# New step lists, thirteen copies on VectorE and an earlier start of the last weight combinations in a fused convolution and SiLU feed-forward kernel

## The chip, the cores and the metric

The kernel runs on one core of a Trainium2 chip. A core has TensorE (matmul), VectorE, ScalarE, GpSimd (here also called Pool) and a queue engine, SyncE (SP), that issues most DMA transfers. Each engine works through its own instructions in program order, and engines wait for one another by semaphores. On-chip memory is SBUF; matmul results land in PSUM, which has eight banks of 128 partitions by 512 fp32 values.

The metric is device time in microseconds (us). A profiled execution is taken by the hardware profiler; its times are those of one run.

## The reference, cut to what matters

```python
# x: (8, 4096, 192), weight: (8, 7), w_in: (192, 2048), w_out: (2048, 192), all fp32
w = softmax(weight, axis=-1)                    # 8 heads of 24 channels, 7 taps
x_pad = concat([zeros(B, 6, D), x], axis=1)
attn[b, s, h, c] = sum_k w[h, k] * x_pad[b, s + k, h*24 + c]
h = attn.reshape(32768, 192) @ w_in
out = (h * sigmoid(h)) @ w_out                  # fp32
```

A causal convolution with seven taps over the sequence, then an up product to 2048 features, SiLU, and a down product back to 192.

## The kernel before, in words

**Blocks.** The 32768 tokens are 32 blocks of 1024, two halves of 512 tokens each. For block b the kernel loads x (`load`, L270), transposes it on VectorE (`turn_in`, L533), gets the six tokens before it (`halo_in`, L548), convolves (`conv`, L561: the first tap on ScalarE, six on VectorE, for each of three groups of 64 channels), spreads the result by DMA into eleven slots of 64 rows on both partition halves (`spread`, L582), and forms sums and differences of slots (`win`, L596).

**Fast matrix products.** Block 0 uses plain matmuls (`up_plain`, `down_plain`). From block 1 on, both products are done with a scheme that needs fewer multiplications. The up product has 20 sub-products for each of four groups g of features (`product`, L644), each an fp32 matmul of 64 rows, 128 columns and 512 tokens; products on the upper and the lower 64 rows of the array (the first number in `PRODUCT`, 0 or 1) run side by side. They add into PSUM banks b0 to b6. Between them stand small steps (`micro`, L659): copies of a bank (kind "c": the u, k and h steps), additions and subtractions (kind "a": j and i steps, VectorE) and SiLU (kind "s": S steps, ScalarE). A copy of kind "c" goes to SBUF (u: a scratch tile; h: a hidden tile) or to another bank (k), and all 44 of a block (eleven kinds, four groups) are ScalarE's. The weights for this scheme are combined once at the start by Pool: `combine((0, 1), e)` and `combine((2, 3), e)` (L464), two groups of features at a time, 28 instructions for each pair of groups.

The down product has 48 slots a block (`out_slot`, L700), D*i*.*je*, each four matmuls on the four 32-column strips of the array, into banks acc0 to acc5. Eight of the 48 (D5) have 128 columns of tokens, the rest 512. Their inputs are hidden tiles and differences of them (`sum_g`, L683, the t steps, VectorE). The accumulators are then merged (`merge`, L769: z, y and x on ScalarE, M on VectorE), transposed (`turn_out`, o) and stored (`store_out`, st).

**The order of the work** is written out in two lists of tokens. `START` covers the first blocks, `PLAN` is one block of steady work and is run through once for each b from 3 to 33. A token names a step and its arguments: P8.2 is product 8 of group 2, D4.31 down slot 4 with j = 3, e = 1, v.26 convolution channel group 2, tap 6. A sign in front shifts the block: "+" is the next block, "-" the one before, "=" two before. `step` (L849) turns a token into its instructions. On each engine the instructions run in the order of the list; the order between engines comes from data alone. A token dp is one step of block 0's plain down product, cp copies its result, go starts the last combination of weights.

**Banks are handed round.** `at` (L257) gives an accumulator the next free bank, scratch tile or t tile when it is first touched, and takes it back after the number of touches in `TOUCHES`. A copy into a new bank can thus have to wait for the step that last read the bank's previous tenant, also where both are ScalarE's.

**The start.** After up_plain, Pool combines groups 0 and 1. The step go then issues a one-element copy out of the convolution tile of block 1 (L886) and, behind it on Pool's queue, the combination of groups 2 and 3. Last, `combine_out` (L476) prepares the down weights. The end (`finish`, L901) is not touched.

Of the kernel before, what the change touches and what calls it, by code (L numbers as in the profile page):

```python
# [17 lines left out]
def kernel(  # L18
# [47 lines left out]
        "ld.1 -st.3 i.1 j10.2 i18_10.2 ld.0 i17_f.2 ld.2 P14.2 t.03 P12.3 ze.0 j10.3 i18_10.3 "  # L66
        "S17.1 P14.3 D4.00 D4.01 D5.00 D1.31 i.0 S16.2 t.10 D5.01 i15_11.2 D3.00 D3.01 t.11 i.2 "
        "ha.0 t.13 i17_f.3 S15.2 t.12 D0.01 D0.21 v.00 t.20 D4.11 D4.10 D3.10 v.10 D2.10 v.20 "
        "v.01 v.11 v.21 S17.2 S18.2 D5.11 D2.11 v.02 t.21 v.22 t.23 v.23 v.03 D0.20 D1.10 D4.20 "
        "v.24 S13.3 i15_11.3 S17.3 D0.30 D4.21 v.04 D2.20 D3.11 D5.10 v.12 v.05 v.25 S15.3 D0.00 "  # L70
        "v.06 D2.21 D0.11 D0.10 t.22 D3.21 v.13 D5.21 D5.20 D0.31 D3.20 S18.3 D1.20 D1.30 D1.21 "
        "sp.0 D1.00 v.26 S16.3 v.14 v.15 z1.0 t.30 v.16 t.32 t.31 t.33 D2.30 D2.31 D5.30 D5.31 "
        "sp.2 y1.0 x2.1 D4.31 y0.0 sp.1 D3.30 D3.31 w.0 x2.2 w.1 w.2 w.3 w.4 x2.3 w.5 y2.0 x2.0 "
        "+P7.1 +P1.0 M1.0 +P7.0 +P1.1 x0.0 +h15.1 +k12.0 D4.30 +h15.0 M3.0 +k12.1 M2.0 x1.0 "
        "+h17.1 +P8.0 +u4.0 +P2.0 +P8.1 +P2.1 +P18.1 +P5.0 M4.0 +u4.1 +P17.1 +P5.1 +j4.0 +k5.0 "
        "+P16.0 +P3.0 +h17.0 M5.0 +k8.0 +P18.0 +P11.0 +P17.0 +S19.1 +k8.1 +P6.0 +u6.0 +h18.0 "
        "+P0.0 +P9.0 +u10.0 +j4.1 +S19.0 +P19.0 +k5.1 +P11.1 +P10.0 +P6.1 +P16.1 M6.0 M7.0 +P3.1 "
# [12 lines left out]
    START = (  # L90
        "-ld.0 =v.20 -ld.2 =v.00 =v.10 =v.01 =v.11 =v.12 =v.13 =dp.0 =dp.1 =dp.2 =dp.3 =dp.4 "
        "-ld.1 =dp.5 =dp.6 =dp.7 =dp.8 =dp.9 =dp.10 =dp.11 =dp.12 =dp.13 =dp.14 =dp.15 =dp.16 "
        "=dp.17 =dp.18 =dp.19 =dp.20 =dp.21 =v.02 =v.21 =dp.22 =v.22 =dp.23 =v.14 =dp.24 =v.23 "
        "=dp.25 =dp.26 =dp.27 =dp.28 =dp.29 =dp.30 =dp.31 =dp.32 =dp.33 =dp.34 =dp.35 =dp.36 "
        "=dp.37 =dp.38 =v.15 =v.03 =v.24 =v.25 =v.26 -i.2 =sp.2 =v.04 =v.05 =v.06 =sp.0 =dp.39 "
        "=dp.40 =dp.41 =dp.42 =dp.43 =dp.44 =dp.45 =dp.46 =v.16 -i.1 =sp.1 =w.1 =w.0 =cp.0 =go.2 "
        "-i.0 =w.2 -ha.0 =w.3 =w.4 =w.5 =dp.47 =cp.1 =o.1 -P1.1 =cp.2 =o.2 -k12.1 -P7.0 -P7.1 "
        "=st.2 -h15.0 -P2.1 -P7.3 -h17.1 -h15.1 -P1.0 -P8.0 -h15.3 -P8.1 -k12.0 -u4.0 -P2.0 "
        "-P17.1 -u4.1 -h17.0 -P5.0 -P18.1 -j4.0 =o.0 -P5.1 -P17.0 -k5.0 -S19.1 -P3.0 -j4.1 -P18.0 "
        "-k8.0 -P11.0 -P16.0 -u6.0 -S19.0 -j6.0 -P9.0 -P8.3 -h18.0 -k8.1 -P6.0 -P0.0 -S14.0 -P6.1 "  # L100
        "-k5.1 -P19.0 -u10.0 -P11.1 -P16.1 -S20.0 -k9.0 -P3.1 -P10.0 -u10.1 -P4.0 -h18.1 -P10.1 "
        "-i15_f.0 -u6.1 -P13.0 -u4.3 -P19.1 -j6.1 -S13.0 -i15_f.1 -P9.1 -P0.1 -k17.0 -k9.1 -j10.0 "
        "-P12.0 =st.1 =st.0 -P7.2 -S14.1 -S20.1 -P13.1 -P15.0 -i17_f.0 -h15.2 -P4.1 -S17.0 -P8.2 "
        "-i18_10.0 -k17.1 -P1.2 -S13.1 -P14.0 -j10.1 -u4.2 -P12.1 -P15.1 -k12.2 -i15_11.0 -S18.0 "
        "-P5.2 -j4.2 -h17.2 -i17_f.1 -P1.3 -S15.0 -P17.2 -i18_10.1 -S16.0 -P2.2 -k8.2 -P18.2 "
        "-t.00 -k12.3 -P6.2 -P14.1 -S17.1 -j4.3 -h17.3 -P11.2 -t.01 -S16.1 -P18.3 -P2.3 -S19.2 "
        "-u10.2 -P17.3 -i15_11.1 -P5.3 -k5.3 -t.03 -P10.2 -k5.2 -P3.3 -S19.3 -P16.3 -k8.3 "
        "-i15_f.2 -P3.2 -P16.2 -h18.3 -P11.3 -u6.2 -P0.3 -P6.3 -h18.2 -u6.3 -P0.2 -P9.2 -u10.3 "
        "-P19.2 -P9.3 -t.02 -j6.2 -j6.3 -k9.2 -S14.2 -P10.3 -k9.3 -P13.2 -S20.2 -P19.3 -S14.3 "
        "-P13.3 -i15_f.3 -k17.2 -P4.2 -S20.3 -P15.2 -k17.3 -P12.2 -v.00 -P15.3 -j10.2 -S13.2 "  # L110
        "-v.01 -S15.1 -D3.01 -i18_10.2 -v.10 -D4.01 -i17_f.2 -v.20 -v.11 -D1.01 -S18.2 -S17.2 "
        "-v.02 -D1.21 -j10.3 -D0.20 -v.03 -i18_10.3 -D0.10 -t.10 -S18.3 -D1.11 -v.12 -D0.00 -v.21 "
        "-D0.11 -v.13 -D1.31 -v.22 -v.14 -P14.2 -P4.3 -v.23 -P14.3 -P12.3 -S16.2 -v.15 -S13.3 "
        "-D1.20 -v.24 -S16.3 -S18.1 -i17_f.3 -D4.00 -v.16 -S17.3 -D3.00 -t.11 -sp.1 -D1.30 -ze.0 "
        "-i15_11.2 -D2.11 ld.1 -i15_11.3 -S15.2 -D2.01 -v.25 -S15.3 -D5.00 -v.04 -D5.01 -D0.21 "
        "-t.12 -D0.30 -D2.00 -t.13 -D2.10 -t.20 -D4.10 -v.05 -D3.10 -t.21 -D4.11 -v.06 -D5.11 "
        "-D5.10 -D2.20 -t.23 -sp.0 -D3.11 -v.26 -D4.20 -t.30 ld.0 -D5.21 -D5.20 -D4.21 -t.31 "
        "-D2.21 -t.22 -sp.2 -D2.31 -t.33 -D1.10 -D3.20 -t.32 ld.2 -D0.01 -D3.31 -w.0 -D5.30 "
        "-D3.30 -w.1 -D4.30 -w.2 -D0.31 i.2 -D3.21 -z1.0 -y0.0 -D5.31 -D1.00 -x0.0 -x2.3 -w.3 "
        "-w.4 -w.5 -D2.30 -y1.0 -x2.1 -D4.31 -x2.0 -M1.0 -x2.2 -M2.0 P7.1 P1.0 -x1.0 -M3.0 h15.1 "  # L120
        "-M4.0 k12.0 P1.1 P7.0 P8.1 -M5.0 h15.0 P2.0 -M7.0 k12.1 P8.0 -o.1 P2.1 h17.1 u4.0 -o.3 "
        "P18.1 u4.1 P5.0 j4.0 -st.3 P17.1 j4.1 h17.0 k5.0 P5.1 P17.0 S19.1 P3.0 -st.1 i.1 k8.0 "
        "P16.0 -y2.0 P11.0 k8.1 P18.0 -M6.0 h18.0 P11.1 u10.0 P19.0 u6.0 P6.0 u10.1 P10.0 P9.0 "
        "S19.0 j6.0 P10.1 k5.1 i15_f.0 P6.1 S14.0 P0.0 -o.0 k9.0 P3.1 i15_f.1 -st.0 P7.3 S20.0 "
        "P13.0 u6.1 P16.1 h15.3 P4.0 j6.1 k17.0 P7.2 h18.1 P9.1 j10.0 S13.0 P19.1 P12.0 k9.1 "
        "S14.1 P15.0 P13.1 h15.2 i17_f.0 P0.1 i18_10.0 P4.1 S17.0 k17.1 P8.2 P1.2 S13.1 j10.1 "
        "P14.0 S20.1 P12.1 u4.2 P15.1 k12.2 i15_11.0 P1.3 S18.0 i17_f.1 P8.3 P5.2 S16.0 i18_10.1 "
        "h17.2 P2.2 u4.3 P14.1 k12.3 P5.3 i.0 -o.2 ha.0 P17.2 k8.2 i15_11.1 h17.3 P2.3 P18.2 j4.2 "
        "S18.1 -st.2 P11.2 S16.1 P18.3 j4.3 S19.2 t.12 P6.2 k5.3 P17.3 u10.2 P3.3 P16.3 k5.2 "
        "S19.3 P3.2 P16.2 u6.3 h18.3 P9.3 P10.2 k8.3 u6.2 P19.3 P6.3 i15_f.2 h18.2 j6.2 S15.1 "  # L130
        "P9.2 P0.3 S15.0 j6.3 P11.3 P0.2 k9.2 t.00 S14.2 P4.2 P19.2 u10.3 t.01 S20.3 P13.2 P10.3 "
        "S20.2 S13.2 t.03 k17.2 D1.31 k9.3 D0.01 j10.2 S14.3 D0.00 v.10 i15_f.3 v.20 t.02 P15.2 "
        "P13.3 v.11 S17.1 D0.11 i18_10.2 D4.01 k17.3 j10.3 S18.2 D4.00 v.21 v.12 D0.10 v.22 D1.01 "
        "v.13 P15.3 P12.3 v.23 P14.2 i18_10.3 v.00 P4.3 i17_f.3 P12.2 P14.3 S16.2 v.14 S17.3 "
        "D2.00 S16.3 i15_11.2 S13.3 i17_f.2 D2.01 S15.2 ze.0 S17.2 D3.00 t.10 S18.3 D5.01 D5.00 "
        "D1.30 t.11 D3.01 t.13 D2.11 D2.10 t.20 D4.11 t.21 D5.11 D4.10 v.24 D3.10 t.23 D0.30 v.25 "
        "D4.20 i15_11.3 D2.21 v.26 S15.3 t.22 D1.20 sp.2 D0.31 v.01 v.15 D3.21 v.02 D3.20 v.16 "
        "D5.21 D4.21 v.03 sp.1 v.04 D2.20 v.05 D3.11 t.32 D1.21 D5.10 v.06 D5.20 D1.10 w.0 sp.0 "
        "t.30 D1.00 D0.21 t.31 D0.20 t.33 D2.31 y0.0 z1.0 D2.30 w.1 D5.31 w.2 D4.31 M1.0 D4.30 "
# [99 lines left out]
    def pin(ins):  # L239
        return tc.keep_in_program_order(ins)  # L240
# [866 lines left out]
```

## Time and profile before

| what | value |
|---|---|
| median of 3 runs | 2387.37 us (2387.32 to 2387.93) |
| profiled execution | 2387.99 us, span 2386.2 us, granted clock 0.997 |
| TensorE busy | 2371.9 us (99%) |
| VectorE busy | 1975.9 us (83%) |
| ScalarE busy | 1459.4 us (61%) |
| Pool busy | 96.5 us (4%) |
| one block, 1213 to 1286 us | TensorE 73.00, VectorE 61.19, ScalarE 45.91, Pool 0.97 us |

In the views, PE is TensorE, PEld its weight load, DVE VectorE, ACT ScalarE. A row names the source line, the engine, the operation, what it writes and reads by the program's names, and shapes; "x" is a count. PSUM banks are all called ps. Every fp32 matmul appears as two records, one for each pass. A line such as L247 is that of a helper that many steps share. TensorE's busy time counts a matmul from its modelled start to its end, so that neighbours overlap.

### The profile page before, as it was taken

How to read it: one execution, taken by the hardware profiler on the slowest of the kernel's cores; microseconds unless marked ns; L12 is line 12 of the kernel's file. 1: busy time of each engine (PE TensorE's matmuls, PEld its weight loads, DVE VectorE, ACT ScalarE, POOL GpSimd, SP SyncE). 2: the span in 40 equal slices, each digit the busy share in tenths (PEclk: the TensorE clock that was granted, in tenths of full speed). 3: DMA queues.
4: the chain of work that ended last, by engine and by line, in shares of the span. 5: the costliest groups of instructions: out<-in, count | busy, mean ns of one | idle time of the engine just before them, and what ended most of it. 6: DMA issues, size and time to landing. Idle time of an engine off the chain costs nothing.

```text
span 2386.2 us, 43893 instructions
## 1 busy us (share of the span) xinstructions
PE 2371.9 (99%) x17382; PEld 1007.4 (42%) x17382; DVE 1975.9 (83%) x2691; ACT 1459.4 (61%) x2833; POOL 96.5 (4%) x129
## 2 busy tenths in 40 slices
PE   9899999999999999999999999999999999999998
PEld 5344443444434444334444344443344443444434
DVE  8777788888889888888888898888888888988886
ACT  5267655577655676555766556665567655577654
POOL 4710000000000000000000000000000000000000
PEclk9999999999999999999999999999999999999999
DMA  7211222212212122122122121221221221212211
GB/s 155 60 34 23 44 44 42 52 28 52 43 34 52 33 46 52 34 43 52 28 52 42 36 52 30 50 51 33 45 50 30 52 40 37 52 28 52 51 31 22
DMA packets 451246, 106.55 MB, mean 45 GB/s; under 512 B 423584, under 2 KB 428704, under 8 KB 451040
## 3 DMA queue, kind: packets, MB, share of 16 engines
q1 hardware_dynamic: 447392, 101.78, 22.7%
q8 instruction: 136, 2.23, 0.4%
q0 software_dynamic: 448, 1.58, 0.3%
q10 hardware_dynamic: 3200, 0.39, 0.1%
q14 instruction: 70, 0.57, 0.1%
HBM read 31.46 MB, written 25.17 MB: 24 GB/s over the span
## 4 chain that ended last, share of the span: by engine, by line
PE 95%; DVE 3%; POOL 1%; ACT 0%; issue 0%; DMA 0%; SPq 0%; DVEq 0%; ACTq 0%; POOLq 0%
PE ps L730 47%; PE ps L649 47%; DVE two L247 1%; DVE nat L570 1%; DVE mh L247 1%; POOL w_own L247 0%; POOL w_other L247 0%; DMA dup<-nat 0%; SPq L279 0%; ACT g L675 0%; DMA nat<-in_x_dram 0%; DVE xt L536 0%; DVE wo L247 0%; ACT ps L673 0%; ACT ps L671 0%
## 5 line engine op out<-in xcount | busy, mean ns | idle before, releaser
L730 PE MATMUL ps<-g,wo 128*32 128x512 f32 x2976 | 692.0, 592 | 0.0
L649 PE MATMUL ps<-win,w_own 64*128 64x512 f32 x1488 | 675.0, 605 | 4.6 <-POOL w_own L247 4.6
L730 PE MATMUL ps<-t,wo 128*32 128x512 f32 (+2 forms) x4528 | 539.6, 446 | 0.0
L649 PE MATMUL ps<-dup,w_other 64*128 64x512 f32 x1240 | 508.7, 602 | 0.0
L730 PE MATMUL ps<-t,wx 128*32 128x512 f32 x2976 | 490.4, 594 | 0.0
L649 PE MATMUL ps<-dup,w_own 64*128 64x512 f32 x1240 | 486.7, 603 | 0.1
L649 PE MATMUL ps<-win,w_other 64*128 64x512 f32 x992 | 472.9, 607 | 2.4 <-DVE win L600 2.4
L678 DVE TENSOR_TENSOR g<-g,ps 128x512 f32<-128x512 f32 x496 | 335.3, 682 | 130.8 <-PE ps L649 126.1
L675 ACT ACTIVATE g<-ps 128x512 f32<-128x512 f32 x620 | 365.5, 602 | 78.6 <-PE ps L649 78.5
L570 DVE SCALAR_TENSOR_TENSOR nat<-xt,turned,nat 128x512 f32<-128x512 f32 x558 | 390.0, 748 | 1.3
L678 DVE TENSOR_TENSOR ps<-u,ps 128x512 f32<-128x512 f32 x372 | 254.4, 685 | 161.8 <-PE ps L649 117.1
L675 ACT ACTIVATE g<-g 128x512 f32<-128x512 f32 x372 | 222.2, 634 | 220.9 <-DVE g L678 220.9
L649 PEld LDWEIGHTS ps<-win,w_own 64*128 64x128 f32 x1488 | 254.9, 187 | 193.7 <-issue 83.8
L695 DVE TENSOR_TENSOR t<-g,t 128x1024 f32<-128x1024 f32 x248 | 301.6, 1217 | 14.6 <-PE ps L730 9.9
L695 DVE TENSOR_TENSOR t<-g 128x1024 f32<-128x1024 f32 x248 | 297.5, 1209 | 5.7 <-PE ps L730 5.7
L730 PEld LDWEIGHTS ps<-t,wo 128*32 128x32 f32 x4528 | 179.6, 110 | 238.7 <-issue 209.8
L649 PEld LDWEIGHTS ps<-dup,w_own 64*128 64x128 f32 x1240 | 188.4, 186 | 185.6 <-issue 73.1
L673 ACT ACTIVATE ps<-ps 128x512 f32<-128x512 f32 x372 | 221.9, 598 | 37.1 <-DVE g L678 15.9
L730 PE MATMUL ps<-g,wx 128*32 128x512 f32 x1488 | 241.5, 594 | 0.0
L730 PEld LDWEIGHTS ps<-t,wx 128*32 128x32 f32 x2976 | 115.9, 110 | 261.5 <-issue 239.1
L649 PEld LDWEIGHTS ps<-dup,w_other 64*128 64x128 f32 x1240 | 192.2, 186 | 77.6 <-issue 27.4
L649 PEld LDWEIGHTS ps<-win,w_other 64*128 64x128 f32 x992 | 170.5, 187 | 114.7 <-issue 62.2
(90 smaller groups left out, 1793.8 us busy)
## 6 DMA issues: line engine op xcount, KB each, us to landing
dup<-nat SPq DMA_DIRECT2D x221, 128.0 KB, 2.3
nat<-in_x_dram SPq DMA_DIRECT2D x382, 64.0 KB, 2.4
out_dram<-t SPq DMA_DIRECT2D x372, 64.0 KB, 2.0
win<-nat SPq DMA_DIRECT2D x124, 128.0 KB, 2.3
raw<-in_moe_w_out_dram SPq DMA_DIRECT2D x8, 384.0 KB, 4.1
raw<-in_moe_w_in_dram SPq DMA_DIRECT2D x12, 192.0 KB, 4.9
w_other<-w_own POOLq DMA_DIRECT2D x8, 192.0 KB, 5.6
raw<-in_moe_w_in_dram SPq DMA_DIRECT2D x6, 128.0 KB, 3.0
```

Of the source, the lines that this page charges most:

```text
L247: return lambda *args, **kw: pin(getattr(self.engine, name)(*args, **kw))
L570: nc.vector.scalar_tensor_tensor(out=dst, in0=src, scalar=tap, in1=dst, op0=ALU.mult, op1=ALU.add)
L649: nc.tensor.matmul(at(b, "bank", to, g), raw(g, w, e), rows(slot_of(b, x_), e), start=first, stop=True, skip_group_check=True,)
L673: pin(nc.scalar.activation(seen[to], seen[u], AF.Copy, scale=-1.0))
L675: pin(nc.scalar.activation(seen[to], seen[u], AF.Silu, scale=float(sign)))
L678: pin(nc.vector.tensor_tensor(seen[to], seen[u], seen[v], op=op))
L695: pin(nc.vector.tensor_tensor(t[i // 2][:, i % 2, :], u, v, op=ALU.subtract))
L730: nc.tensor.matmul(acc[SQ * q : SQ * q + SQ, to], lhs[:, e, SQ * k : SQ * k + SQ], rhs[:, e, ts(q, TB // 4) if i == 5 else to], start=firs ...
```

## The change

1. `PLAN` and `START` are other lists. PLAN holds the same 311 tokens (shifts aside) in another order; START has 927 tokens where it had 879. The change's own words are that the lists are laid out with ScalarE's waits on its own reads.
2. A new tuple `ON_DVE` names 13 of the 44 copies of kind "c"; these are issued on VectorE, as a `tensor_copy`, or as a `tensor_scalar` with -1 where the sign is negative.
3. The step go no longer has the one-element copy, and stands behind dp.12 in START, where it stood behind cp.0.

The lists, cut to the parts that the prediction speaks of:

```diff
     PLAN = (
-        "ld.1 -st.3 i.1 j10.2 i18_10.2 ld.0 i17_f.2 ld.2 P14.2 t.03 P12.3 ze.0 j10.3 i18_10.3 "
...
-        "sp.2 y1.0 x2.1 D4.31 y0.0 sp.1 D3.30 D3.31 w.0 x2.2 w.1 w.2 w.3 w.4 x2.3 w.5 y2.0 x2.0 "
-        "+P7.1 +P1.0 M1.0 +P7.0 +P1.1 x0.0 +h15.1 +k12.0 D4.30 +h15.0 M3.0 +k12.1 M2.0 x1.0 "
-        "+h17.1 +P8.0 +u4.0 +P2.0 +P8.1 +P2.1 +P18.1 +P5.0 M4.0 +u4.1 +P17.1 +P5.1 +j4.0 +k5.0 "
...
-        "+P12.2 +k17.3 +P15.3 +t.00 +S20.3 +S17.0 +S20.2 +P4.2 +t.01 +D1.11 +D2.01 +S13.2 +S15.1 "
-        "+D1.01 +D2.00 +S18.1 +P4.3"
+        "ld.2 i.2 ld.0 i.0 ld.1 i.1 t.12 D4.11 D5.11 D3.10 t.20 t.21 ha.0 v.00 D0.21 v.20 v.01 "
...
+        "v.25 v.04 v.05 v.06 t.23 v.15 t.22 v.16 D4.20 D4.21 t.30 D3.21 v.26 D5.20 sp.1 t.31 "
+        "D2.31 D3.20 D2.30 sp.2 t.32 t.33 D5.31 D5.30 w.0 sp.0 w.2 z1.0 D5.21 w.3 D4.31 D3.31 "
+        "D3.30 y1.0 x2.1 w.1 M1.0 D4.30 w.4 +P7.0 x2.2 w.5 y2.0 x0.0 y0.0 +P1.1 +P7.1 x1.0 +h15.0 "
+        "+P1.0 +P8.0 M3.0 M2.0 +k12.1 +P2.1 +k12.0 x2.0 +h15.1 +P8.1 +h17.1 +P2.0 M4.0 +u4.0 "
...
+        "+S15.1 +P4.3 +j10.2 +P15.3 +i17_f.2 +i15_f.3 +D2.01 +D0.11 +D4.00 +P12.3 +S13.3 +S18.1 "
+        "+i18_10.2 +P14.2 +j10.3 +P4.2 +ze.0 +i18_10.3 st.0 +P14.3 +S17.1 +D5.00 +S17.2 +D5.01 "
+        "+t.10 +i15_11.2 +D4.01 +i17_f.3 +D2.00 +S18.2 +t.11 +D3.01 +i15_11.3 +t.13 +D2.10 +S13.2 "
+        "+D3.00 +D4.10 +D1.11 +D1.01 +S17.3 +D2.11 +D1.00 +S18.3 +D0.20 +D1.21 +S15.3 +D0.01 "
+        "+D1.30 +D0.10 +S15.2 +D1.31 +D0.30 +D1.10 +D0.31 +D0.00 +S16.2 +D1.20"
     )
     START = (
...
-        "=dp.40 =dp.41 =dp.42 =dp.43 =dp.44 =dp.45 =dp.46 =v.16 -i.1 =sp.1 =w.1 =w.0 =cp.0 =go.2 "
-        "-i.0 =w.2 -ha.0 =w.3 =w.4 =w.5 =dp.47 =cp.1 =o.1 -P1.1 =cp.2 =o.2 -k12.1 -P7.0 -P7.1 "
-        "=st.2 -h15.0 -P2.1 -P7.3 -h17.1 -h15.1 -P1.0 -P8.0 -h15.3 -P8.1 -k12.0 -u4.0 -P2.0 "
...
+        "-ld.2 -ld.0 =dp.0 -ld.1 =dp.1 =dp.2 =dp.3 =dp.4 =dp.5 =dp.6 =dp.7 =dp.8 =dp.9 =dp.10 "
+        "=dp.11 =dp.12 =go.2 =v.10 =dp.13 =dp.14 =dp.15 =dp.16 =dp.17 =dp.18 =dp.19 =dp.20 =dp.21 "
...
+        "=sp.1 =sp.0 =dp.41 =dp.42 =w.0 =dp.43 =w.1 =dp.44 =w.2 =dp.45 =w.3 =w.4 =dp.46 =cp.0 "
+        "=w.5 =dp.47 =cp.1 =o.0 -P7.0 =o.1 =st.1 -P1.1 =cp.2 -k12.1 -P7.1 -P1.0 -h15.0 -h17.1 "
...
     )
+    ON_DVE = ('h15.2', 'h15.3', 'h17.0', 'h17.1', 'h17.3', 'h18.2', 'k12.0', 'k12.1', 'k5.3', 'u10.0',
+              'u10.3', 'u6.0', 'u6.1')
...
-        if kind == "c":
+        if kind == "c" and f"{name}.{g}" in ON_DVE:
+            if sign > 0:
+                pin(nc.vector.tensor_copy(seen[to], seen[u]))
+            else:
+                pin(
+                    nc.vector.tensor_scalar(
+                        seen[to], seen[u], scalar1=-1.0, scalar2=None, op0=ALU.mult
+                    )
+                )
+        elif kind == "c":
...
         elif name == "go":
-            pool.tensor_copy(warm, nats[1][:, digits[0], 0, 0:1])
             for e in range(2):
                 combine((2, 3), e)
```

## The prediction

> **What bounds the kernel now.** I read the page's busy times first, then the chain that ended last.
>
> ```profile
> PE 2371.9 (99%) x17382; PEld 1007.4 (42%) x17382; DVE 1975.9 (83%) x2691; ACT 1459.4 (61%) x2833; POOL 96.5 (4%) x129
> PE 95%; DVE 3%; POOL 1%; ACT 0%; issue 0%; DMA 0%; SPq 0%; DVEq 0%; ACTq 0%; POOLq 0%
> ```
>
> TensorE is the chain, but 99% busy only says that it always has a matmul open. So I read the chain in order of time over one block, columns start, duration, what:
>
> ```profile
> 1177.23 1.92 PE ps L649 x8
> 1179.14 31.93 PE ps L730 x344
> 1211.07 1.92 PE ps L649 x8
> 1212.99 1.00 PE ps L730 x8
> 1213.98 32.68 PE ps L649 x142
> 1246.66 3.57 PE ps L730 x32
> ```
>
> A block (1024 tokens) repeats every 73.01 us (1173.66 to 1246.66). L649 are the 80 up products, L730 the 48 down slots, and TensorE changes between them six times a block. How fast it can go is in its timeline:
>
> ```profile
> 1213.91 0.69 PE L649 MATMUL ps<-win,w_other 64*128 64x512 f32 x1
> 1214.45 0.59 PE L649 MATMUL ps<-win,w_other 64*128 64x512 f32 x1
> 1214.88 0.59 PE L649 MATMUL ps<-win,w_other 64*128 64x512 f32 x1
> ...
> 1220.52 0.69 PE L649 MATMUL ps<-dup,w_other 64*128 64x512 f32 x1
> 1221.05 0.59 PE L649 MATMUL ps<-dup,w_own 64*128 64x512 f32 x1
> ```
>
> An undisturbed pass starts 0.43 after the one before; a product is two passes, and two products run side by side on the two row halves. 80 products are 80 x 0.4275 = 34.2 us; 40 full down slots at 0.855 are 34.2; the 8 short ones at 0.22 are 1.8. **Floor 70.2 us of 73.0.** A pass of 0.69 marks a weight load that was not ready: its successor comes 0.53 later, so each late start costs its wait plus 0.11. Entering the products costs 0.11 + 0.11, leaving them 0.10 + 0.03 (1246.07, 1246.59, 1247.05 in the timeline): 0.35 a pair, and three pairs are 1.05. The other 1.8 us are late products: the stretch of 72 takes 32.68 where 36 pairs need 30.8. What they wait for is mostly ScalarE's copies (waits of the weight loads: ACT g L671 77.7 us, ACT ps L673 73.6). ScalarE's timeline shows one reason:
>
> ```profile
> 1217.75 0.61 ACT L671 COPY ps<-ps 128x512 f32<-128x512 f32 x1
> 1218.26 0.61 ACT L675 ACTIVATE g<-ps 128x512 f32<-128x512 f32 x1
> 1218.90 0.57 ACT L671 COPY ps<-ps 128x512 f32<-128x512 f32 x1
> ```
>
> Copies follow one another every 0.48, but S19.1 at 1218.26 reads a bank that k8.1 at 1218.90 overwrites, so k8.1 waits for ScalarE's own read: 0.64. I count eight such steps in the block, about 0.16 each. Stages by engine:
>
> ```profile
> 1213.00:1286.00 73.00, 73.00 (x548) 30.44 (x552) 61.19 (x84) 45.91 (x90) 0.97 (x1) 1.00 0.23 43
> ```
>
> VectorE 61.2, ScalarE 45.9 of 73.0. That leaves VectorE 11.8 us a block without work. At the start, three timelines: Pool idles 13.35 us, its weights done, until VectorE's convolution is through:
>
> ```profile
> 89.86 0.19 POOL L247 COPY warm<-nat 128x1 f32<-128x1 f32 x1 [13.35 <-DVE nat L570]
> ```
>
> VectorE's convolution steps, first with Pool idle, then with Pool at work:
>
> ```profile
> 79.66 9.98 DVE L570 SCALAR_TENSOR_TENSOR nat<-xt,turned,nat 128x512 f32<-128x512 f32 x14
> ...
> 90.31 4.38 DVE L570 SCALAR_TENSOR_TENSOR nat<-xt,turned,nat 128x512 f32<-128x512 f32 x4
> ```
>
> And the products that wait for those weights:
>
> ```profile
> 112.25 1.22 PE L649 MATMUL ps<-win,w_own 64*128 64x512 f32 x1 [4.61 <-POOL w_own L247]
> ```
>
> **The change part by part.** Same steps, same 128 TensorE steps a block; the floor stays.
>
> *Fewer changes of kind.* Read cyclically, the old PLAN's TensorE steps go P4 D43 P4 D1 P72 D4, the new one P76 D3 P4 D45. One pair less: -0.35 us a block. PLAN does products for blocks 4 to 31, 28 times: -9.8. START has one run of products more (7 for 6), +0.35.
>
> *Late products.* For each product I followed the steps it waits for back to the TensorE step that released them, added the rows (copy spaced 0.48, VectorE add 0.60, a matmul's end to a start 0.16 + 0.07, hand-over to the weight load 0.05, the load 0.19) and set that against the TensorE work between. In the old list the late ones hang at the end of long ScalarE queues: P0.0 0.57 (ten steps behind x1.0), P15.2 0.65 (some thirty steps back, with P19.2 and P10.3 on the way). With 0.11 for each of seven late starts that is 2.0, where the trace has 1.7: this way of counting is 15% high. In the new list the chains are three to seven steps: P8.0 0.31 (x0.0, y0.0, x1.0 at 0.60 and h15.0 must fit behind D3.30, with D4.30 and four products, 2.57 us, to cover them), P12.2 0.22, P15.1 0.09, D0.11 0.05, P10.3 0.04: 0.71, with four late starts 1.15, less 15% 1.0. Steps of ScalarE directly behind their own read fall from seven in the list to four. So 1.7 to 1.0: -0.7 a block, 28 x 0.7 = -19.6. Bounds: nothing gained (the deficits only change names), or all 1.7 gone.
>
> *Thirteen copies to VectorE.* ScalarE loses 13 x 0.48 = 6.2 (to 39.7). No row has VectorE copying 128x512 from PSUM. Nearest are its additions that read PSUM (busy 0.685, spaced 0.60); the ends are 0.48, ScalarE's spacing, and 0.745, the convolution step. I take 0.60, the same reads and output size: +7.8, VectorE 69.0 of some 72 (67.4 to 70.9). Its cover is TensorE's stretch, and it is thin: in the list's 76 products (32.5 us) VectorE has 50 steps, 32.1 us; before it had 31, 20.2. Queued behind such a copy are the additions j, i, and fillers t, v. I cost it at nothing beyond the chains above, because the 13 down slots D2.11 to D1.20 carry almost no VectorE work in the list, and it can run 10 us ahead there. [...]
>
> *DMAs moved.* sp.0's four spreads now stand behind sp.2's, directly ahead of w.2 on VectorE. SP issues one per 0.64, landing 2.3 later: the eighth lands 6.8 us after v.26, and w.2, w.3, w.4 lose about 1.5 us by it. P7.0 had 1.4 of slack there, so 0 to 0.3 for P1.1; P8.0 then waits less by as much. Zero. The loads ld now come together, with i.2 right behind on VectorE; SP issues them as soon as st.0 is out, and VectorE is ahead there: zero, up to 2 us of VectorE's lead.
>
> *Pool at once.* The copy that made Pool wait is gone, so the last 28 combinations start at 76.5 instead of 90.0. But VectorE's convolution now runs beside them: 4 steps took 4.38 (1.10 each) beside Pool, 14 took 9.98 (0.71) alone. 18 x 1.10 = 19.8 from 79.7 gives 99.5; the last spreads land about 104, the windows are ready at 105.3 to 107.5, say 106.4, and Pool is done at about 105. Before, products started at 103.45, four ran, and the rest waited until 112.25, then ran at half rate to about 116.7 (granted clock 0.66 in 110 to 120). Now there is one cold start, not two: four products by 110.2, warm soon after. Gain 2 to 6, I take -3. The other end: if every convolution step lost a whole Pool step (0.71 + 1.05), it would end at 111.4, products start at 119, a loss of 9. [...] The row of 1.10 lies nearer 0.71, so I go by the row.
>
> Sum on the profiled run (span 2386.2, 2387.99 with what lies around it, 0.6 over the median): -9.8 - 19.6 + 0.4 - 3 = -32.0, so 2356.0; against the median 2355.4. I round up for P1.1 and say **2357**.
>
> **Rivals.** *The stalls stay*: only the changes of kind and the start pay, -12.4, 2375. For it: P8.0 is now worse than it was (0.31 for 0.07). Against: the queues behind the worst ones are gone. *Nearly all stalls go*: 28 x (0.35 + 1.6) + 3 - 0.4 = 57.2, 2330; against: P8.0 and P12.2 can't be met by these rows. [...] *VectorE becomes the bound*, the one that ends slower: it idles 11.8 us a block today, nearly all waiting for products or ScalarE (4.0 on g, 4.8 on ps, 2.4 on cmb), and with 69.0 of work it may idle only 4.0. If half of today's idling stays, a block is 69.0 + 5.9 = 74.9, +1.9 x 28 = +53, 2440. It decides from 4.0 us of idling. For it: 50 steps beside 76 products. Against: ten of the thirteen copies (u, h15, h17, h18) are read next by an addition on VectorE itself, so a hand-over goes with each.
>
> **How the numbers follow.** My forecast 0.45 (2345 to 2369), stalls stay 0.17, nearly all go 0.12, the lock 0.06, VectorE bound 0.16, within 0.2% 0.04 (some 5 us either way, what a measurement of this kernel can tell from no change). Faster 0.80, same 0.04, slower 0.16. The range 2330 to 2384 leaves out VectorE's case and little else.
>
> **What would show it.** The chain with four pieces a block, not six: one product stretch of about 34 us, and a period near 72.0. VectorE near 69 and ScalarE near 40 in 73 us; 0.69 passes at P8.0 and P12.2 and few elsewhere. Pool's combinations from 76.5 with no wait of 13.3, convolution steps near 1.1, and one idle gap of TensorE between 101 and 107. Wrong would be: VectorE's idling above 4 us with TensorE waiting for its copies (then slower), a copy above 0.75, or windows later than 112.

## The result and the profile after

The kernel after takes 2411.45 us (median of 4 runs, 2410.29 to 2414.25), the kernel before 2387.65 (4 runs, 2387.32 to 2388.00): 1.0101 times as long, 95% interval 1.0084 to 1.0119. It is slower by 1%, where 2357 was forecast.

The page of the kernel after (span 2408.6, its run 2410.29), busy times and the chain that ended last:

```profile
PE 2359.9 (98%) x17382; PEld 971.7 (40%) x17382; DVE 2219.7 (92%) x3094; ACT 1288.4 (53%) x2430; POOL 103.4 (4%) x128
PE 60%; DVE 27%; SPq 4%; issue 4%; DMA 4%; ACT 1%; DVEq 0%; ACTq 0%
```

Before, 95% of the chain was TensorE. Now VectorE holds 27%, and SP's issues and DMA transfers, which stood at 0%, hold 4% each. The place shows in the chain in order of time (start, duration, what) over one block, from the first product of one block to that of the next:

```profile
1225.03 23.64 PE ps L655 x104
1248.66 0.67 DVE g L693
...
1275.43 4.74 DVE nat L576 x7
...
1286.11 0.67 DVE nat L576
...
1286.85 0.48 SPq L595
...
1293.16 3.29 DMA win<-nat
...
1296.54 0.15 DVE dup L606
...
1297.14 0.68 DVE cmb L825
1297.85 0.59 ACT yx L810
...
1298.56 1.52 PE ps L655 x4
```

TensorE leads for 23.6 us of products. Then the chain goes over to VectorE and stays in its queue for 38 us (additions, differences of hidden tiles, transposes, convolution), without a wait for TensorE. It goes on through eleven spreads that SP issues one after another, the landing of the last, a window, M1.0, y2.0 and only then the next block's first product. A block's period is that loop, not TensorE's work.

Three blocks in the view by windows (window: length, then busy time and count of TensorE, its weight load, VectorE, ScalarE, Pool; granted clock, DMA share, GB/s):

```profile
1152.45:1225.03 72.58, 72.36 (x545) 29.08 (x545) 68.86 (x97) 40.41 (x77) 0.97 (x1) 1.00 0.23 43
1225.03:1298.56 73.53, 72.35 (x544) 29.06 (x545) 68.84 (x97) 40.40 (x77) 0.97 (x1) 1.00 0.23 42
1298.56:1372.71 74.15, 72.36 (x544) 29.04 (x545) 68.85 (x97) 40.40 (x77) 0.97 (x1) 1.00 0.23 42
```

The engines' work is the same in each; only the length varies, 72.5 to 75.2. The mean from block 6 to block 31 is 73.43 (492.81 to 2328.46, 25 periods), 73.01 before. What lies between, on SP and on VectorE in the second of these blocks (columns: start, duration, engine, line, what; a count; in brackets the idle time before and what ended it):

```profile
1286.85 0.48 SPq L595 DMA_DIRECT2D dup<-nat  x1
1287.44 1.18 SPq L595 DMA_DIRECT2D win<-nat  x2
1288.67 3.81 SPq L595 DMA_DIRECT2D dup<-nat  x6
1292.57 2.12 SPq L595 DMA_DIRECT2D win<-nat  x2
```

```profile
1287.83 0.75 DVE L576 SCALAR_TENSOR_TENSOR nat<-xt,turned,nat 128x512 f32<-128x512 f32 x1
...
1292.83 1.53 DVE L606 TENSOR_TENSOR dup<-dup 128x512 f32<-128x512 f32 x2 [0.78 <-DMA dup<-nat]
1295.93 0.69 DVE L606 TENSOR_TENSOR win<-dup,win 128x512 f32<-128x512 f32 x1 [1.56 <-DMA win<-nat]
```

The last convolution step (v.26) ends at 1288.58. The eight spreads of sp.2 and sp.0 go out behind it, the last lands at 1296.45, 7.9 us later, and VectorE waits 2.3 us for them in front of the windows. In the block before, where no issue takes longer than the others, the last one lands 6.9 us behind v.26 (1222.94 for 1216.00) and VectorE waits 1.5. In the kernel before, VectorE goes from its last t step into the windows without a wait:

```profile
1204.17 2.55 DVE L695 TENSOR_TENSOR t<-g,t 128x1024 f32<-128x1024 f32 x2
1206.64 1.88 DVE L600 TENSOR_TENSOR dup<-dup 128x512 f32<-128x512 f32 x3
```

The copies that VectorE took over, beside an addition:

```profile
1247.06 0.68 DVE L677 COPY g<-ps 128x512 f32<-128x512 f32 x1
1247.66 0.69 DVE L693 TENSOR_TENSOR ps<-u,ps 128x512 f32<-128x512 f32 x1
```

They cost 0.68 to 0.70 busy and follow at 0.60, as an addition does.

At the start, VectorE's convolution of block 1 beside Pool, and the first product:

```profile
81.06 19.73 DVE L576 SCALAR_TENSOR_TENSOR nat<-xt,turned,nat 128x512 f32<-128x512 f32 x18
```

```profile
108.16 1.19 PE L655 MATMUL ps<-win,w_own 64*128 64x512 f32 x1 [6.16 <-DVE win L606]
```

Last, where START hands over to PLAN, VectorE's timeline:

```profile
303.89 2.59 DVE L693 TENSOR_TENSOR g<-g,ps 128x512 f32<-128x512 f32 x4 [3.21 <-PE ps L655]
311.95 1.23 DVE L710 TENSOR_TENSOR t<-g,t 128x1024 f32<-128x1024 f32 x1 [5.47 <-PE ps L745]
...
318.03 1.23 DVE L710 TENSOR_TENSOR t<-g 128x1024 f32<-128x1024 f32 x1 [1.94 <-PE ps L745]
...
320.50 10.52 DVE L576 SCALAR_TENSOR_TENSOR nat<-xt,turned,nat 128x512 f32<-128x512 f32 x15
```

The steps t.13 and t.20 each write one of three t tiles, and a tile is free only when the down slots that read its previous tenant are through. START's last part has D2.00 and D3.00, the last readers, near its end. Two waits of 5.5 and 1.9 us follow, with 15 convolution steps of block 4 queued behind them, and the first product of block 4 comes at 346.17, where it came at 334.95.

So the difference of the two spans, +22.4 us, can be followed from one start of the product stretch to the next. The kernel after is 4.7 late at block 1 (108.16 for 103.45), 1.1 early at block 2 (185.95 for 187.06), 0.5 early at block 3 (260.74 for 261.23) and **11.2 late at block 4**. It loses **another 11.1 over the 27 periods to block 31**, and nothing after it.

### The profile page after: what moved, and what is told of

Read it like the earlier page. It is cut to its first block, busy times and chain, and to the rows that moved or that the text cites. A ratio compares the mean times of both kernels' runs of the same rounds, so it can differ in the third digit from the quotient of the medians.

```text
span 2408.6 us, 43750 instructions
## 1 busy us (share of the span) xinstructions
PE 2359.9 (98%) x17382; PEld 971.7 (40%) x17382; DVE 2219.7 (92%) x3094; ACT 1288.4 (53%) x2430; POOL 103.4 (4%) x128
## 4 chain that ended last, share of the span: by engine, by line
PE 60%; DVE 27%; SPq 4%; issue 4%; DMA 4%; ACT 1%; DVEq 0%; ACTq 0%
PE ps L655 39%; PE ps L745 21%; DVE nat L576 9%; DVE t L710 8%; SPq L595 4%; DVE g L693 3%; DMA win<-nat 3%; DVE ps L693 2%; DVE two L253 1%; DVE xt L542 1%; DVE cmb L825 1%; ACT yx L810 1%; DVE mh L253 1%; DVE ps L680 0%; DVE g L677 0%
## 5 line engine op out<-in xcount | busy, mean ns | idle before, releaser
L655 PE MATMUL ps<-win,w_own 64*128 64x512 f32 x1488 | 661.0, 600 | 34.4 <-ACT yx L810 24.7
L745 PE MATMUL ps<-g,wo 128*32 128x512 f32 x2976 | 682.4, 592 | 0.0
L745 PE MATMUL ps<-t,wo 128*32 128x512 f32 (+1 forms) x4528 | 533.1, 448 | 6.1 <-DVE t L710 6.1
L655 PE MATMUL ps<-dup,w_own 64*128 64x512 f32 x1240 | 516.1, 594 | 0.0
L655 PE MATMUL ps<-dup,w_other 64*128 64x512 f32 x1240 | 499.4, 597 | 0.0
L576 DVE SCALAR_TENSOR_TENSOR nat<-xt,turned,nat 128x512 f32<-128x512 f32 x558 | 398.2, 760 | 6.8 <-ACT nat L573 2.6
L693 DVE TENSOR_TENSOR g<-g,ps 128x512 f32<-128x512 f32 x496 | 321.4, 678 | 25.2 <-PE ps L655 23.2
L710 DVE TENSOR_TENSOR t<-g 128x1024 f32<-128x1024 f32 x248 | 298.5, 1213 | 11.3 <-PE ps L745 11.1
L655 PEld LDWEIGHTS ps<-dup,w_own 64*128 64x128 f32 x1240 | 200.8, 186 | 139.0 <-issue 82.8
L655 PEld LDWEIGHTS ps<-win,w_other 64*128 64x128 f32 x992 | 176.5, 188 | 139.4 <-issue 70.2
L745 PEld LDWEIGHTS ps<-g,wo 128*32 128x32 f32 x2976 | 172.9, 110 | 147.8 <-issue 143.2
L688 ACT ACTIVATE ps<-ps 128x512 f32<-128x512 f32 x341 | 200.6, 589 | 46.2 <-PE ps L655 22.9
```

What stands on the lines that cost most here:

```text
L576: nc.vector.scalar_tensor_tensor(out=dst, in0=src, scalar=tap, in1=dst, op0=ALU.mult, op1=ALU.add)
L655: nc.tensor.matmul(at(b, "bank", to, g), raw(g, w, e), rows(slot_of(b, x_), e), start=first, stop=True, skip_group_check=True,)
L688: pin(nc.scalar.activation(seen[to], seen[u], AF.Copy, scale=-1.0))
L693: pin(nc.vector.tensor_tensor(seen[to], seen[u], seen[v], op=op))
L710: pin(nc.vector.tensor_tensor(t[i // 2][:, i % 2, :], u, v, op=ALU.subtract))
L745: nc.tensor.matmul(acc[SQ * q : SQ * q + SQ, to], lhs[:, e, SQ * k : SQ * k + SQ], rhs[:, e, ts(q, TB // 4) if i == 5 else to], start=firs ...
```

## The experiments

Two readings of the profile compete. One is the order: the spreads stand too late in a loop without slack, and START leaves PLAN a late join. The other is the amount: VectorE has become the bound, as in the rival that was given 0.16.

Block starts are those of the first product in each profiled run; "mean period" is from block 6 to block 31. Edits of the lists are cut to the tokens that move. Ratios are to the kernel before, in brackets the 95% interval.

### Parts of the change alone, and undone

**b_dve**: the kernel before's lists, with the thirteen copies on VectorE.

```diff
+    ON_DVE = ('h15.2', 'h15.3', 'h17.0', 'h17.1', 'h17.3', 'h18.2', 'k12.0', 'k12.1', 'k5.3', 'u10.0',
+              'u10.3', 'u6.0', 'u6.1')
...
+        if kind == "c" and f"{name}.{g}" in ON_DVE:
```

> The kernel before with its own lists, and only the 13 copies moved to VectorE. Theory 1: VectorE has 69 us of work a block and its old waits of 11.8 can't all be taken in; the period rises above 73, 2400 to 2480 us. Rival (VectorE has room, each copy is hidden): 2380 to 2392 us.

Measured: 2443.08 us, 1.0231 (1.0216 to 1.0246). From 1213 to 1286 us VectorE is busy for 67.05 of 73.00 and ScalarE for 39.82; the chain by engine:

```profile
PE 80%; DVE 18%; POOL 1%; issue 1%; SPq 0%; DMA 0%; ACT 0%; DVEq 0%; ACTq 0%; POOLq 0%
```

Moved without a new list, the copies cost 55 us: 8.7 until block 4 starts (343.67 for 334.95), and 1.67 for each period behind it (74.68 for 73.01). VectorE works 68.7 us of such a period, and it holds 18% of the chain. SP and DMA have no share in it: this is another loss than that of the kernel after.

**b_go**: the kernel before's lists, with Pool's early start alone.

```diff
         elif name == "go":
-            pool.tensor_copy(warm, nats[1][:, digits[0], 0, 0:1])
```

(and =go.2 moved from behind =cp.0 to behind =dp.12)

> The kernel before with its own lists, and only the start of the last weight combinations changed: no copy ahead of them, and the step behind dp.12. If the gain at the start of the changed kernel (first long run of products at 108.2 instead of 112.3 us) comes from Pool alone and lasts: 2383 to 2386 us. If Pool beside the convolution only delays the windows by as much (the lock): 2387 to 2395 us.

Measured: 2387.54 us, 0.9998 (0.9989 to 1.0007). The convolution steps beside Pool take 1.08 (14 in 15.17 us), and the first product comes at 110.37, where in the kernel before four came at 103.45 and the rest at 112.25. Block 2 starts at 186.55 (187.06 before), block 3 at 260.85 (261.23): of the 1.9 us that the long run of products gains, 0.4 are left at block 3. The second expectation holds. What it calls the lock, in the prediction the case that every convolution step loses a whole Pool step (0.71 + 1.05 = 1.76), is not what the row of 1.08 shows.

**a_nodve**: the kernel after with all 44 copies on ScalarE.

```diff
-    ON_DVE = ('h15.2', 'h15.3', 'h17.0', 'h17.1', 'h17.3', 'h18.2', 'k12.0', 'k12.1', 'k5.3', 'u10.0',
-              'u10.3', 'u6.0', 'u6.1')
+    ON_DVE = ()
```

> The changed kernel with all 44 copies back on ScalarE; lists and Pool's start stay as changed. Theory 1 (VectorE carries the block: 68.9 us of work and 3.7 to 5.3 us of waits in 72.5 to 74.2): VectorE falls to about 61 us a block, runs ahead again in the down slots, the spreads start earlier, and the period goes to TensorE's 71.5 to 72.6: 2365 to 2390 us in all (the one late block near 300 us may stay). Theory 2 (the order of the spreads and windows alone, the copies cost nothing): the period stays near 73.4, 2403 to 2413 us.

Measured: 2545.09 us, 1.0665 (1.0649 to 1.0681), far from every figure expected: the mean period is 78.01 us. VectorE's work falls to 61.3 us a block, and ScalarE's rises to 46.5. The waits (what waited, for what: us in total, times, longest us):

```profile
PEld ps L654 <- ACT u L685: 89.7, 157, 1.2
DVE ps L692 <- ACT u L685: 88.8, 65, 4.1
```

The new order of the products needs copies sooner than ScalarE's queue delivers them: products and VectorE's additions wait for its u copies. Because of this new loss the run cannot tell whether VectorE's amount of work slows the kernel after; a_light and a_vfirst below can. It shows, with b_dve, that lists and copies are one edit. Either alone loses.

**a_poolonly**: the kernel after with Pool's copy back and go behind cp.0.

```diff
-        "=dp.11 =dp.12 =go.2 =v.10 =dp.13 ..."
+        "=dp.11 =dp.12 =v.10 =dp.13 ..."
...
-        "... =dp.46 =cp.0 =w.5 =dp.47 ..."
+        "... =dp.46 =cp.0 =go.2 =w.5 =dp.47 ..."
...
         elif name == "go":
+            pool.tensor_copy(warm, nats[1][:, digits[0], 0, 0:1])
```

> The kernel after with Pool's one-element copy back and go behind cp.0, and nothing else moved: only the third part of the change is undone. Theory (beside Pool the eighteen convolution steps of block 1 take 19.7 us, with Pool waiting 12.0 as in a_latepool, and the products of groups 0 and 1 need no more of Pool): the first product starts at about 101 instead of 108.2, the join and the windows cost what they cost in the kernel after, 2411.5 - 8 = 2403. Rival (what is gained at block 1 is taken up by the late join at block 4): 2410 to 2412.

Measured: 2408.66 us (2406.03 to 2409.00), 1.0081 (1.0068 to 1.0095), between the two expectations. The first product comes at 101.44, as the theory says, and block 4 starts at 340.10, 6.1 sooner than in the kernel after. But from block 4 to block 31 this execution takes 1987.4 us, where the kernel after takes 1982.3, with the same list, so most of the 6.1 is lost again. The periods of a loop that the windows set scatter (last section); whether this loss is chance or a consequence, the run cannot tell. The intervals of the two kernels overlap, so the 2.8 us between their medians are not clear of noise.

### The steady blocks: where the spreads stand

**a_sp0**: one token of PLAN moved.

```diff
-        "v.25 v.04 v.05 v.06 t.23 v.15 t.22 v.16 ... v.26 D5.20 sp.1 t.31 "
-        "D2.31 D3.20 D2.30 sp.2 t.32 t.33 D5.31 D5.30 w.0 sp.0 w.2 ..."
+        "v.25 v.04 v.05 v.06 sp.0 t.23 v.15 t.22 v.16 ... v.26 D5.20 sp.1 t.31 "
+        "D2.31 D3.20 D2.30 sp.2 t.32 t.33 D5.31 D5.30 w.0 w.2 ..."
```

> The changed kernel with one token moved in PLAN: sp.0 right behind v.06, ahead of sp.1 and sp.2; copies stay on VectorE. Theory 2 (eleven spreads in one row behind v.16, at 0.64 us each, hold up the windows and with them the first products): four of eleven issues leave the row, the last landing comes about 2 us earlier, the period falls by 0.8 to 1.5 us, 2368 to 2390 us. Theory 1 alone (VectorE's work is the bound, its wait at the windows only moves to another place): at most 0.3 us a block, 2401 to 2412 us.

Measured: 2374.50 us (2372.20 to 2376.61), 0.9943 (0.9927 to 0.9960). One token is worth 37 us and turns the kernel after into one faster than before. The mean period falls from 73.43 to 72.11, and seven of the 25 periods are 71.64 long or a hundredth less, which no block of the kernel after reaches. Block 4 still starts at 345.66.

**a_light**: the kernel after with two convolution steps of VectorE left out.

```diff
+        if b >= 4 and k == 0 and i in (3, 4):
+            return
         src = xts[b][:, k, i : i + TB]
```

> The kernel after with two of VectorE's convolution steps (taps 3 and 4 of channel group 0) left out from block 4 on, so the output lacks those two taps: 1.34 us of VectorE a block, all of it ahead of the spreads. Theory A (the path of a block runs through VectorE's unbroken queue, then the eleven spreads, then the windows): every us taken off VectorE comes off the period until TensorE's own 71.64 is reached, 73.43 to about 72.2, so 2411.5 - 28 x 1.2 = 2378. Theory B (SP's issues and the banks alone make the windows late, VectorE's amount does not matter): under 5 us of change, 2407 to 2412.

Measured: 2388.07 us (2384.72 to 2390.73), 0.9998 (0.9989 to 1.0008), a gain of 23.4: less than theory A's 33, far more than theory B's 5. The mean period is 72.69, 0.74 less for 1.34 less work. VectorE's waits from block 6 to block 31 tell why not all of it arrives, first those of the kernel after, then those of a_light (what waited, for what: us in total over 25 periods, times, longest us):

```profile
DVE dup L606 <- DMA dup<-nat: 31.8, 47, 1.8
DVE win L606 <- DMA win<-nat: 24.8, 28, 2.3
```

```profile
DVE t L712 <- PE ps L747: 32.9, 50, 0.9
DVE win L608 <- DMA win<-nat: 24.8, 27, 2.8
DVE dup L608 <- DMA dup<-nat: 15.7, 30, 1.3
```

VectorE comes sooner to its last t steps and then waits there for down slots, 1.3 us a block, which it does not do in the kernel after. It waits less for the spreads, but still 1.6 us a block where it was 2.3. Both links of the loop count: VectorE's unbroken queue ahead of the spreads, and the row of spreads behind it, which still keeps the period above 71.64.

**a_vfirst**: all convolution ahead of the t steps, each group's spreads directly behind its last tap, and the join of START and PLAN moved as in a_joinonly below.

```diff
-        "v.25 v.04 v.05 v.06 t.23 v.15 t.22 v.16 D4.20 D4.21 t.30 D3.21 v.26 D5.20 sp.1 t.31 "
-        "D2.31 D3.20 D2.30 sp.2 t.32 t.33 D5.31 D5.30 w.0 sp.0 w.2 ..."
+        "v.25 v.04 v.05 v.06 sp.0 v.15 v.16 sp.1 v.26 sp.2 t.23 t.22 D4.20 D4.21 t.30 D3.21 "
+        "D5.20 t.31 D2.31 D3.20 D2.30 t.32 t.33 D5.31 D5.30 w.0 w.2 ..."
```

> The kernel after with the join moved as in a_joinonly, and with PLAN's order v.06 sp.0 v.15 v.16 sp.1 v.26 sp.2 ahead of t.23, t.22 and the D steps that followed, where sp.1, sp.2 and sp.0 stood behind t.23, t.22, t.30, t.31. Theory (each block loses what the windows are late by the time of the last spread): the last spread is issued some 3 us sooner than with sp.0 alone moved, nearly all blocks run at the undisturbed 71.64 us that half of them had there, so 2374.5 - 8 (join) - 9 = 2357 to 2360. Rival (the remaining half microsecond a block comes from y2.0, which ScalarE can read only behind M1.0's read of the same bank): only the join pays, 2366.

Measured: 2356.47 us (2356.22 to 2358.72), 0.9869 (0.9854 to 0.9883), as the theory says, half a microsecond under its range. Mean period 71.73, 19 of 25 below 71.75. In VectorE's timeline the windows follow the last t step without a wait:

```profile
1267.18 1.22 DVE L712 TENSOR_TENSOR t<-g,t 128x1024 f32<-128x1024 f32 x1
1268.31 1.41 DVE L608 TENSOR_TENSOR dup<-dup 128x512 f32<-128x512 f32 x2
1269.76 0.69 DVE L608 TENSOR_TENSOR win<-dup,win 128x512 f32<-128x512 f32 x1
```

VectorE is as busy as before the move (68.94 in the 71.63 us from 1201.78 to 1273.41), so VectorE, 96% busy, is not the bound of this kernel.

**a_y2**: a_sp0 with the join moved and y2.0 ahead of M1.0.

```diff
-        "D3.30 y1.0 x2.1 w.1 M1.0 D4.30 w.4 +P7.0 x2.2 w.5 y2.0 ..."
+        "D3.30 y1.0 y2.0 x2.1 w.1 M1.0 D4.30 w.4 +P7.0 x2.2 w.5 ..."
```

> The kernel after with sp.0 behind v.06, the join moved as in a_joinonly, and y2.0 moved ahead of w.1 and M1.0, directly behind y1.0, so that M1.0 is the last to read the bank and ScalarE's copy no longer stands between M1.0 and the first product. Theory (spread order): the windows stay as they were with sp.0 moved, so only the join pays, 2374.5 - 8 = 2366, less a little. Rival (the hand-over M1.0, y2.0, first product costs the disturbed blocks their 0.6): the first product starts about 0.7 us sooner in those, 2366 - 28 x 0.4 = 2355.

Measured: 2367.41 us (2366.73 to 2371.42), 0.9916 (0.9901 to 0.9931). The mean period is 72.15, as in a_sp0 (72.11), so the row "ACT yx L810" in the chain is a station on the way and no cause; the 7.1 us are the join's. **a_best**, a_vfirst with the same move of y2.0, agrees:

> a_vfirst with y2.0 moved ahead of w.1 and M1.0 as in a_y2. Theory (in a_vfirst the windows are no longer late, so nothing between VectorE's merge and the first product is left to gain but in the few blocks of 71.7 to 72.5): the mean period goes from 71.73 to 71.65, 2356.5 - 2 = 2354. Rival (y2.0's hand-over still costs in every block): 2345.

Measured: 2357.45 us (2356.85 to 2358.00), 0.9872 (0.9856 to 0.9889), no different from a_vfirst.

### The start

**a_joinonly**: the kernel after with two tokens of START moved, so that the t tiles come free sooner.

```diff
-        "+S17.2 +D0.00 +ze.0 ... +D2.01 +j10.3 ... +S13.2 +D3.01 +D1.31 "
-        "+D1.11 +D1.10 +D2.00 +D0.30 ... +D1.01 +D3.00 +D2.11 +t.13 +D4.10 +D0.01"
+        "+S17.2 +D0.00 +ze.0 ... +D2.01 +D2.00 +j10.3 ... +S13.2 +D3.01 +D3.00 +D1.31 "
+        "+D1.11 +D1.10 +D0.30 ... +D1.01 +D2.11 +t.13 +D4.10 +D0.01"
```

> The kernel after, with two tokens moved in the last part of START: D2.00 directly behind D2.01 and D3.00 directly behind D3.01, so that two t tiles come free before VectorE reaches the steps t.13 and t.20. The order of the spreads stays as in the kernel after. Theory (two separate losses: a late join of START and PLAN, once, and late windows in each block): VectorE's waits of 5.5 and 1.9 us at 312 and 318 us go, the product stretch of block 4 starts 7 to 9 us sooner, and the period stays at 73.4: 2411.5 - 8 = 2403. Rival (VectorE's full queue, not the tiles, delays block 4): the stretch starts as late as before and the time stays at 2411.

Measured: 2407.45 us (2401.31 to 2411.87), 1.0078 (1.0061 to 1.0096). The two waits of 5.5 and 1.9 us are gone, and blocks 3 to 4 take 78.66 us instead of 85.43, so the join is the cause there; blocks 2 to 3 took 2.7 more in this execution, and 3.4 arrive at block 4 (342.76). The mean period stays at 73.44. The medians differ by 4.0, half of what was expected, with overlapping intervals. In the pair a_sp0 and a_y2, with fewer late windows, the move is worth the 7.1.

**a_latepool**: a_vfirst, with Pool waiting for the convolution again (the edit of a_poolonly).

> a_vfirst with Pool's one-element copy back and go behind cp.0, so that the last combinations wait for VectorE's convolution as in the kernel before. Theory (what the early start of Pool gains at block 1 is given back by block 3 or 4, as with the kernel before's own lists, where it was worth 0.1): 2356.5, within 2 us. Rival (with the new START list the 3.5 us at block 1 stay): 2360.

Measured: **2347.74 us** (2346.68 to 2349.73), 0.9832 (0.9818 to 0.9847). Both expectations missed: Pool's early start is neither worth nothing here nor a gain. Without it the kernel is 8.7 us faster, and it is the fastest of all. VectorE and TensorE at the start, in their timelines:

```profile
79.80 12.01 DVE L578 SCALAR_TENSOR_TENSOR nat<-xt,turned,nat 128x512 f32<-128x512 f32 x18
```

```profile
97.49 3.60 PE L766 MATMUL ps<-g,wo 128*64 128x512 f32 x16
101.03 0.69 PE L657 MATMUL ps<-win,w_own 64*128 64x512 f32 x1
```

With Pool waiting, the 18 steps take 12.0 us for 19.7, and the windows are done just as block 0's plain down product ends. TensorE goes from the one to the other without a gap and at full rate: its granted clock is 1.00 from 100 to 120 us, and passes take 0.59 to 0.69 from the start. In the kernel after, behind the gap of 6.2 us, the granted clock is 0.50 from 108.16 to 112.40, and passes take 1.06 to 1.22. No product waits for Pool, although it starts its last combinations at 91.82: the new START takes the products of groups 0 and 1 first. P7.3, a product of the last group of features, stood fifth among block 1's products in the old START and stands 35th in the new one; P1.2, eighth in the new one, shows no wait for Pool. The hole from 103.45 to 112.25 in the kernel before came from that place in the list, and the new list closes it by itself. The chain of this kernel over a block:

```profile
1261.51 33.37 PE ps L657 x152
1294.87 2.71 PE ps L747 x24
1297.59 1.92 PE ps L657 x8
1299.50 33.64 PE ps L747 x360
```

It is TensorE alone, in four pieces.

**a_oldstart**: a_vfirst with the kernel before's START (go behind dp.12, no copy of Pool's), 48 steps appended that the new PLAN expects done, and the copies of blocks 1 to 3 on ScalarE.

```diff
-        if kind == "c" and f"{name}.{g}" in ON_DVE:
+        if kind == "c" and f"{name}.{g}" in ON_DVE and b > 3:
```

> a_vfirst with the kernel before's START, go behind dp.12 and without Pool's copy, the 48 steps that the new PLAN expects to be done already appended in PLAN's own order, and blocks 1 to 3 with all copies on ScalarE. Theory (the new START is slower than the old one from block 1 to block 4, 231.8 us in a_vfirst for 222.8 in the kernel before): the stretch of block 4 starts at 335 instead of 340.5, 2356.5 - 5 = 2351. Rival (the loss lies in going over to the new PLAN, whatever START is): 2357 to 2362.

Measured: 2354.91 us (2354.45 to 2356.03), 0.9862 (0.9847 to 0.9877), 1.6 less than a_vfirst where 5 were expected. Block 4 starts at 338.21 (340.49 in a_vfirst), with the first product at 110.49. The going over from START to PLAN costs about the same with either list: blocks 3 to 4 take 76.53 here, 77.67 in a_vfirst and 73.72 in the kernel before. The old START is hardly better than the new one.

| kernel | median us | ratio to before | block 1 | block 4 | mean period |
|---|---|---|---|---|---|
| before | 2387.65 | | 103.45 | 334.95 | 73.01 |
| after | 2411.45 | 1.0101 | 108.16 | 346.17 | 73.43 |
| a_poolonly | 2408.66 | 1.0081 | 101.44 | 340.10 | 73.63 |
| a_joinonly | 2407.45 | 1.0078 | 107.95 | 342.76 | 73.44 |
| a_light | 2388.07 | 0.9998 | 107.91 | 343.09 | 72.69 |
| a_sp0 | 2374.50 | 0.9943 | 108.17 | 345.66 | 72.11 |
| a_y2 | 2367.41 | 0.9916 | 107.94 | 338.83 | 72.15 |
| a_vfirst | 2356.47 | 0.9869 | 108.70 | 340.49 | 71.73 |
| a_latepool | 2347.74 | 0.9832 | 101.03 | 329.87 | 71.69 |

## Why the prediction was wrong, point by point

**The floor and *Fewer changes of kind*: right.** The chain of a_latepool has four pieces a block. Where the windows are on time a period is 71.64: 70.2 of work, 0.70 for two pairs of changes, and 0.74 that is left.

***Late products*: right, a little too cautious.** The 0.74 is the term forecast at 1.0, and the two products that it named first are late indeed. In a_latepool's block from 1189.76, apart from the two entries into products, passes of 0.69 come at 1191.76 and 1221.25, by their places in the list P8.0 and P12.2, and at 1195.27, about P16.0, which was not foreseen. With the windows on time the steady part is 35.3 us shorter than before (1935.9 for 1971.2 in a_latepool, blocks 4 to 31), where the two steps together promised 29.4.

***Thirteen copies to VectorE*: the price right, the cover wrong.** 0.60 for each, VectorE at 68.85 (forecast 69.0), ScalarE at 40.4 (39.7). A copy is busy for 0.68 to 0.70; the list pays the 0.60 at which the copies follow. What failed is the sentence that VectorE "can run 10 us ahead" in the down slots. The chain shows it at work without a break from 1248.7 to the windows' doorstep: it has no lead there, and what it gains or loses ahead of the spreads moves the next products (0.74 us of the 1.34 in a_light).

***DMAs moved*: the step that failed.** It was priced at zero, on slack that only that lead would have given. Its own figure was near: it had the eighth spread landing 6.8 us behind v.26, where 6.9 were measured in one block and 7.9 in the next. But it then set the delay of w.2 to w.4 against 1.4 of slack at P7.0, and did not ask whether the products themselves begin only when those windows are through. In the kernel after they do, and M1.0 and y2.0 stand between: in the 22 blocks from 6 to 31 for which the trace has the last spread's landing, it comes 0.9 to 2.5 us ahead of the first product, where it is 3.8 to 5.5 in a_vfirst. By a_sp0 this is 37 us; by a_vfirst, less the 7.1 of the join, 48. It is more than the whole gain that was forecast.

***START*: left out.** The term was +0.4, for one more run of products. What the last part of START leaves for PLAN's first block to wait for (t tiles, in this case) was never looked at; it is 7.1 us between a_sp0 and a_y2, and 4.0 between the medians of the kernel after and a_joinonly.

***Pool at once*: the rate right, the sign wrong.** The convolution took 19.73 (19.8 forecast), the first product came at 108.16 (106.4 forecast). But the forecast compared it with the old list's hole. In the new list the hole is gone without it, and the early start costs 8.7 us in a_latepool's comparison. In the kernel after itself only 2.8 of that show in the medians, and these are not clear of noise.

**The rivals.** VectorE as the bound, given 0.16, is nearest. Its condition holds (idle for 73.43 - 68.85 = 4.6, over the 4.0 from which it decides), but not its price (+0.4 a block, not +1.9), and its mechanism only in part: of the 4.6 us, 2.3 are waits for spreads, of which the kernel before had none and a_vfirst has 0.1, and 1.2 are waits for products, of which a_vfirst still has 1.1. The mechanism as it was priced appears in b_dve, with a period of 74.68 where the rival had 74.9. The lock, given 0.06 and priced at a loss of 9 in place of the gain of 3, is shown by no run: it has each convolution step lose a whole Pool step, 1.76 in all, and a step takes 1.10 beside Pool (18 in 19.73 in the kernel after), against 0.67 in a_latepool (18 in 12.01). Strict turns of the two engines do not agree with the trace either (figures in the last section).

In sum: -29.4 was right for the steady blocks, with 35.3 to be had, and what took it back was the place of three tokens that issue DMAs and of the convolution's last steps ahead of them, the join of two lists, and an early start that had lost its purpose.

## What to carry to other kernels

When an engine goes from 84% to 94% busy, price what it holds up and not only what it does: look for the DMA issues that follow its last step before a barrier, and put each directly behind the step that it needs. Where a list written for the steady state is joined to one for the start, follow the buffers over the seam. A wait that was harmful under one order of work may protect something under another; undo it together with the order, not by itself.

## What was not expected of the hardware

- Eleven spreads of 128 KB leave SP in 6.9 us when nothing disturbs (0.64 each), but in eleven of 26 blocks (6 to 31) one issue among them takes 0.7 to 1.4 us longer (the last pair 2.12 instead of 1.19 in the block shown). In seven more no issue is that late, but a spread lands 3.4 to 4.4 us after its issue instead of 2.3. Both go with a packet of another queue. The DMA queues (packets, MB, share of 16 engines) during the row of the block from 1152.45 (1214.28 to 1222.94), then of the block from 1225.03 (1286.85 to 1296.45):

```profile
q1 hardware_dynamic: 880, 1.44, 71.5%
```

```profile
q1 hardware_dynamic: 880, 1.44, 64.7%
q8 instruction: 1, 0.02, 0.8%
q14 instruction: 1, 0.01, 0.2%
```

The profile gives q8 the kind "instruction"; its packets are 16 KB. Such a packet starts during the row in exactly those 18 blocks, and the products of these come 73.3 to 75.2 us after those of the block before. In the other eight they come after 72.5 to 72.8. So the order alone costs about 1.0 us a block over 71.64, and the delays another 0.8, because the loop has no slack for them. With the spreads ahead of the t steps (a_vfirst) ten rows still have such a late issue, but 19 of 25 periods stay below 71.75. That the packet itself holds the spread up is not shown: no run moves it.
- VectorE and Pool slow one another, here without taking turns in full: beside each other, 18 convolution steps of 1.10 and some 16 Pool steps of about 1.17 fit into 19.7 us (the kernel after, from 81.06); at their undisturbed 0.67 (a_latepool, 18 steps in 12.01) and 0.73 (the kernel before from 106 to 114 us, where VectorE has no work) they would take 23.7 one after the other.
